# Attention heads and a long convolution in one stream of instructions: another way to order the halves of the fill products, other turns for them, other transfers and another prologue

## The chip, the core and the metric

The kernel runs on one core of a Trainium2 chip. The core has engines that each work through their own list of instructions: TensorE (PE in the profile, with its weight loads as PEld), VectorE (DVE), ScalarE (ACT) and GpSimd (POOL). SyncE (SP) issues transfers; POOL issues some too. The metric is the time of one execution on the device in microseconds (us). Three runs of the kernel before took 1076.99, 1078.38 and 1080.54 us, so the median is 1078.38 us.

## What is computed

There are two independent parts, and the output (1 x 2048 x 1024) is their concatenation. Part A is attention with 32 query heads of 16 dimensions that share one head of keys and values. Part B multiplies a short causal convolution of k (4 taps) by v, applies a causal convolution of length 2048 per channel by a Fourier transform, and gates the result by q. Cut to what matters:

```
# A: x (1,2048,512), wq, wo (512,512), wk, wv (512,16)
q = (x @ wq).reshape(B, S, H, Dh).transpose(0, 2, 1, 3)     # H = 32, Dh = 16
k, v = x @ wk, x @ wv
scores = einsum("bhqd,bkd->bhqk", q, k) * Dh ** -0.5
o = einsum("bhqk,bkd->bhqd", softmax(scores), v)
a = o.transpose(0, 2, 1, 3).reshape(B, S, H * Dh) @ wo
# B: q, k, v (1,2048,512), shift_k (512,4), ssm_k (512,2048), ssm_D (512)
k_shift = sum over t of k_pad[:, t:t+S, :] * shift_k[:, 3 - t]
kv = k_shift * v
y = irfft(rfft(kv, 4096) * rfft(ssm_k, 4096))[:, :2048] + kv * ssm_D
b = q * y
return concatenate([a, b], -1)
```

## The kernel before

The attention sets the frame. Its 32 x 2048 x 2048 scores are cut into 1024 tiles of 128 x 1024, and one tile is one **turn**. 32 turns make a **stack** (4 heads by 512 queries, all keys). In a turn PE makes the scores of a tile (L808: 8 matmuls that use two row halves and four column groups of the array, with 49 rows of contraction: queries in a high and a low part and one row that holds an upper bound of the score), and ACT takes their exponential (L820, `exp`) from a PSUM tile `s` of two banks into SBUF (`p`, 7 buffers). `s` has two buffers. The product with the values (PV, L840, `pv`) comes once in two turns, with 16 matmuls in f32, and adds up in two PSUM banks over a stack. `plan()` fixes the turn of each PV. At a stack's start it delays the first ones: the PV of the first four key pairs stand in four consecutive turns, after four turns without any.

Everything else is **fill**: the query projections, the Fourier products of part B and the output projection. Each is a Python generator (a thread), and `_Fill.turn` decides in each turn of the written program how many fill products PE gets, from the constants `SLOT` (the length of a turn, 916 ns), `SCORES`, `PV`, `UNIT` (prices of the parts) and `LATE` (how far PE may fall behind, 340 ns). The order in which the program is written is the order on each engine; no scheduler changes it.

Fill products run in pairs by `halves()` (L208): one product of a pair uses the upper 64 rows of the array, the other the lower 64, and each writes one of two PSUM banks (pool `pf`, four single banks). Halfway the two change banks. The second half must not write a bank before the last product of the first half has. Before the change the exponential of the next turn carries that wait, so that the PE work of a later turn, which follows that exponential, is ordered too:

```
if half == 0:
    self.mark = y                 # L210ff: the last product of the first half
    yield WAIT, 1, CONT
...
if self.mark is not None:         # exp(), L818ff
    self.tc.add_manual_dep(x.ins, self.mark.ins.name, info, reason="row halves change banks")
```

DVE takes the results out of PSUM and does the radix-4 steps of the transform; its instructions stand in the order of the program too. Transfers go out on two issuing engines: POOL for the tables and inputs of part B, SP for the rest (queries to a DRAM scratch `qd` and back as `st`, attention outputs `od`, weights `wof`, the spilled half `xd` of the transposed x). In `conv_load` (L270), SP issues the transposition of the 4 taps, `skd<-in_B_shift_k`, as a transfer of single elements (2048 x 1 x 1, L274), and POOL's `tpb` (L320) reads the result. The 16 spill transfers (L719) stand in a row at the end of the prologue.

The prologue transposes x in four parts (`x_turn`, L521), projects keys and values (`kv`, L543), projects two groups of queries, and makes the score bound for eight heads (`bound`, L653) before the first two turns. `last` (L1007) ends the program with the last PV, the last head's division (`over`) and the remaining output products `x<-wl,lr` (L206).

## Time and profile before

| what | value |
|---|---|
| median of the runs | 1078.38 us |
| the profiled execution | 1078.28 us |
| its span in the trace | 1076.1 us |
| mean granted PE clock | 0.979 |
| PE busy | 959.0 us, 89% of the span |
| DVE busy | 679.5 us, 63% |
| ACT busy | 971.7 us, 90% |
| POOL busy | 170.8 us, 16% |
| DMA packets, volume | 71985, 83.03 MB |

The span is the time between the first and the last instruction that the profile shows; 2.2 us of the execution lie around it. An engine's busy time is a sum over its instructions, and it tells nothing of which wait ended last. "Idle before" in a row is the time that an engine stood still just before these instructions, and the name behind the arrow is what ended it. PEclk is the share of full clock that TensorE was granted.

### The profile page before, as it was taken

Reading aid. Unit: us, or ns where it says so; the run is one execution under the profiler, and the core shown is the slowest. Engines: PE = TensorE matmul, PEld = TensorE weight load, DVE = VectorE, ACT = ScalarE, POOL = GpSimd, SP = SyncE. Lnnn points to the kernel's source line nnn. Section 1 sums busy time; section 2 is a strip of 40 time slices with the busy share of each in tenths; the row PEclk is TensorE's granted clock in tenths of the full one; section 3 lists DMA queues with packets and bytes.
Section 4 is the critical chain, followed back from the end, with each engine's and each line's share of the span. In section 5 each row is a group of like instructions: output and inputs, shape, how many; then the busy total and the mean of one; then the engine's idle time right before and its main releaser. Section 6 shows DMA issues by size and latency. Waiting matters only on the chain.

```text
span 1076.1 us, 50114 instructions
## 1 busy us (share of the span) xinstructions
PE 959.0 (89%) x22903; PEld 453.9 (42%) x22903; DVE 679.5 (63%) x949; ACT 971.7 (90%) x1038; POOL 170.8 (16%) x300
## 2 busy tenths in 40 slices
PE   6875999899999999989999999999787998999896
PEld 4342444444444444434444444444333443444352
DVE  3607767588826888898888551865998893120142
ACT  3655999899999999999999999999999999999994
POOL 3206221400050000001413112311000001310000
PEclk9887999999999999999999999999999999999998
DMA  7365431722251122212404123421101021220101
GB/s 235 104 15 178 148 103 44 156 59 90 70 112 51 50 70 61 61 40 62 133 27 141 60 88 115 124 77 54 40 20 40 21 70 60 88 93 31 50 4 43
DMA packets 71985, 83.03 MB, mean 77 GB/s; under 512 B 23502, under 2 KB 60952, under 8 KB 71768
## 3 DMA queue, kind: packets, MB, share of 16 engines
q1 hardware_dynamic: 49688, 43.50, 14.6%
q0 software_dynamic: 20320, 35.46, 11.4%
q8 instruction: 181, 2.97, 1.2%
q10 hardware_dynamic: 1760, 0.81, 0.3%
q14 instruction: 36, 0.29, 0.1%
HBM read 54.66 MB, written 25.02 MB: 74 GB/s over the span
## 4 chain that ended last, share of the span: by engine, by line
ACT 40%; PE 38%; issue 11%; DMA 5%; DVE 4%; SPq 0%; ACTq 0%; POOL 0%; DVEq 0%
ACT p L820 40%; PE f L840 16%; PE s L808 10%; PE f L223 10%; DMA skd<-in_B_shift_k 3%; PE f L206 1%; DMA od<-ao 1%; DMA rl<-od 1%; DMA wqf<-in_A_wq 1%; DMA tpb<-skd 1%; DVE sp L144 0%; PE x L529 0%; DVE xT L541 0%; PE x L206 0%; DVE t L354 0%
## 5 line engine op out<-in xcount | busy, mean ns | idle before, releaser
L820 ACT ACTIVATE p<-s 128x1024 f32<-128x1024 f32 x1024 | 959.9, 1049 | 71.6 <-PE s L808 33.5
L840 PE MATMUL f<-p,vx 64*32 64x512 f32 (+1 forms) x8448 | 563.4, 585 | 11.8 <-DVE cut L633 9.2
L808 PE MATMUL s<-st,kst 49*32 49x512 f16 x8192 | 444.5, 383 | 80.3 <-ACT p L820 65.5
L808 PEld LDWEIGHTS <-kst 49*32 49x32 f16 x8192 | 197.1, 90 | 470.2 <-issue 431.3
L840 PEld LDWEIGHTS f<-p,vx 64*32 64x32 f32 x8448 | 171.2, 107 | 58.0 <-issue 24.1
L144 DVE TENSOR_TENSOR sp<-sp 128x1024 f32<-128x1024 f32 x96 | 111.6, 1216 | 0.0
L259 DVE COPY sp<-f 128x512 f32<-128x512 f32 x64 | 41.2, 685 | 85.3 <-PE f L223 85.2
L264 POOL DMA_DIRECT2D ff<-in_ff x64 | 34.2, 539 | 259.9 <-PE s L808 251.9
L851 DVE COPY ao<-f 128x512 f32<-128x512 f32 (+1 forms) x33 | 22.2, 674 | 80.0 <-PE f L840 80.0
L428 POOL DMA_DIRECT2D out<-r x32 | 17.3, 544 | 309.8 <-DVE r L426 309.8
L223 PE MATMUL f<-xT,wq 64*32 64x512 f16 x1344 | 56.6, 382 | 2.6 <-DVE gm L668 2.6
L144 DVE TENSOR_TENSOR sp<-sp,sp 128x1024 f32<-128x1024 f32 x48 | 55.9, 1216 | 0.3
L223 PE MATMUL f<-wo,o 64*32 64x512 f16 x1440 | 55.1, 375 | 0.2 <-DVE gm L668 0.2
L426 DVE TENSOR_TENSOR r<-f,q 128x256 f32<-128x256 f32 x32 | 12.1, 420 | 56.4 <-PE f L223 56.4
L223 PE MATMUL f<-a,ff 64*32 64x256 f32 x1024 | 43.7, 376 | 0.2 <-DVE sp L259 0.2
L223 PE MATMUL f<-hT,ff 64*32 64x256 f32 x1024 | 42.1, 376 | 0.7 <-DVE hT L305 0.7
L223 PE MATMUL f<-sp,fi 64*32 64x256 f32 x1024 | 39.2, 375 | 0.0
L363 DVE TENSOR_TENSOR a<-a,t 128x512 f32<-128x512 f32 x48 | 33.2, 691 | 1.5
L354 DVE TENSOR_TENSOR t<-kk,tpb 128x512 f32<-128x512 f32 (+1 forms) x50 | 33.0, 663 | 1.1 <-DMA kk<-in_B_k 1.1
L223 PEld LDWEIGHTS <-wq 64*32 64x32 f16 x1344 | 25.7, 94 | 17.6 <-DVE gm L668 4.1
L345 POOL DMA_DIRECT2D v<-in_B_v x32 | 17.0, 536 | 96.0 <-PE s L808 48.4
L223 PEld LDWEIGHTS <-o 64*32 64x32 f16 x1440 | 23.4, 93 | 14.7 <-issue 3.3
(133 smaller groups left out, 643.1 us busy)
## 6 DMA issues: line engine op xcount, KB each, us to landing
ff<-in_ff POOLq DMA_DIRECT2D x64, 128.0 KB, 2.9
od<-ao SPq DMA_DIRECT2D x60, 128.0 KB
qd<-qp SPq DMA_DIRECT2D x48, 128.0 KB
st<-qd SPq DMA_DIRECT2D x60, 98.0 KB
kk<-in_B_k POOLq DMA_DIRECT2D x32, 128.0 KB, 3.1
v<-in_B_v POOLq DMA_DIRECT2D x32, 128.0 KB, 2.5
hin<-in_B_ssm_k POOLq DMA_DIRECT2D x32, 128.0 KB, 7.4
fi<-in_fi POOLq DMA_DIRECT2D x32, 128.0 KB, 2.8
```

The costliest lines, as they stand in the source:

```text
L144: v.tensor_tensor(part(out), part(a), part(b), op)
L223: y = self.nc.tensor.matmul(out[j : j + 32, cols], w[r, j : j + 32], x[r], start=half == m == 0, stop=half == 1 and m == k - 1,)
L259: self.nc.vector.tensor_copy(c[:, :, m + i, :], b[i].rearrange("p (q n) -> p q n", q=2))
L264: self.nc.gpsimd.dma_start(t[:, i], self.I[n][:, 2 * m2 + i])
L345: nc.gpsimd.dma_start(v[:, i], self.vr[:, 2 * m2 + i, cs])
L354: nc.vector.tensor_tensor(out[:, n], kk[:, x], tap(i, n.stop - n.start), ALU.mult)
L363: nc.vector.tensor_tensor(a, a, t, ALU.add)
L428: nc.gpsimd.dma_start(self.orr[:, 2 * m2 + i, D + blk * CB : D + (blk + 1) * CB], r[:, i])
L808: self.nc.tensor.matmul(s[j : j + 32, e, :], self.kst[rows, k * P + j : k * P + j + 32], self.st[n][rows, a, cols], start=True, stop=True,)
L820: x = self.nc.scalar.activation(self.pt[u], s, AF.Exp, scale=DH**-0.5 / SC / SC)
L840: nc.tensor.matmul(self.acc[e][32 * j : 32 * j + 32, 0:m], self.vx[rows, k, :], y, start=k == 0, stop=k == NKT - 1)
L851: nc.vector.tensor_copy(a, self.acc[0][:, 0:m])
```

## The change

The change has these parts.

- **Halves.** `halves()` no longer sets a mark for the exponential. After the first half it writes a tiny DVE instruction, a memset of a 128 x 4 tile `look`, that waits for the last product of the first half; the first product of the second half waits for the memset. The two banks of a pair now come as one PSUM tile (`pair()`, two buffers in the place of four single banks), and the wait between the halves is one turn in the place of two.
- **Turns.** `LATE` goes from 340 to 200, so a turn with PV has no room for fill. `plan()` puts a stack's first PV two turns late and the second in two parts of 256 columns, one and three turns late. The exponential is written straight behind the scores.
- **Transfers.** The taps are loaded as rows of 128 elements, transposed by a DVE copy and written to `skd` in rows of 32. `ssm_D` comes as 8 rows of 32 with a DVE transposition. The 16 spill transfers become a thread `spill` with one per turn, and the reloads, the loads of part B and those of the heads are spread in the same way; the convolution waits for the end of `spill`.
- **Prologue.** Matmuls of zeros (`warm`) stand at the start and in gaps. PSUM places of the x transposition alternate between both pools. The score bound of the first stack's four heads is written straight into `st` (row 32 of each row half, `first_rows`); only the first 256 keys are prepared before the first scores, and the second group of queries, the keys from 1024 on and the second stack move behind the first turns into `rest_of_q`.

```diff
-SLOT, SCORES, PV, UNIT, LATE = 916, 220, 430, 216, 340
+SLOT, SCORES, PV, UNIT, LATE = 916, 220, 430, 216, 200
...
-LEAD = 44
+LEAD = 30
...
+    def pair(self):
+        return self.pf.tile([P, 2, 512], F32, tag="f", name=self.nm("f"))
     def bank(self):
-        return self.pf.tile([P, 512], F32, tag="f", name=self.nm("f"))
+        return self.pair()[:, 0, :]
+    def order(self, a, b):
+        info = mybir.DependencyInfo(mybir.DependencyClass.Sync, mybir.DependencyReason.DATA)
+        self.tc.add_manual_dep(a.ins, b.ins.name, info, reason="row halves change banks")
...
-        banks = []
+        banks, look = [], None
         for half in range(2):
             n, k = 0, len(a)
             while n < k:
                 g = yield (k - n) * grain, dve * half, CONT if banks else NEW, grain
                 start = not banks
                 if start:
-                    banks += [self.bank(), self.bank()]
+                    f = self.pair()
+                    banks += [f[:, 0, :], f[:, 1, :]]
                 for m in range(n, n + g // grain):
                     for e in range(2):
                         out, (cols, w, x) = banks[half ^ e], (a, b)[half ^ e][m]
@@ -227,10 +236,14 @@
                                 start=half == m == 0,
                                 stop=half == 1 and m == k - 1,
                             )
+                            if look is not None:
+                                self.order(y, look)
+                                look = None
                 n += g // grain
             if half == 0:
-                self.mark = y
-                yield WAIT, 1, CONT
+                look = self.nc.vector.memset(self.look, 0.0)
+                self.order(look, y)
+                yield WAIT, 0.5, CONT
         return banks
...
-        self.dt = self.c.tile([32, 8], F32, name="dt")
+        sk = w.tile([16, 32, 4], F32, tag="s2", bufs=S2, name="sk")
+        nc.sync.dma_start(sk, I["B_shift_k"].rearrange("(c h) t -> c h t", c=16))
         self.skd = self.dr.tile([4, 512], F32, name="skd")
-        nc.sync.dma_start(self.skd, I["B_shift_k"].rearrange("c t -> t c"))
         yield WAIT, 6
+        tps = w.tile([16, 4, 32], F32, tag="s2", bufs=S2, name="tps")
+        yield 0, 200
+        nc.vector.tensor_copy(tps, sk.rearrange("c h t -> c t h"))
+        nc.sync.dma_start(self.skd.rearrange("t (c h) -> c t h", c=16), tps)
...
-        self.nc.sync.dma_start(self.dt, self.I["B_ssm_D"][blk * CB : blk * CB + CB].rearrange("(c p) -> p c", p=32))
...
+            yield WAIT, 1.5
...
+        d = [self.s2("d", (32,)) for _ in range(2)]
+        nc.gpsimd.memset(d[0][0:32], 0.0)
+        nc.sync.dma_start(d[0][0:8], self.I["B_ssm_D"][blk * CB : blk * CB + CB].rearrange("(c p) -> c p", p=32))
         yield WAIT, 4
-        yield 0, 200
-        d = hin[0:32, :, 0:1]
-        nc.vector.tensor_tensor(d, d, self.dt.unsqueeze(2), ALU.add)
+        yield 0, 400
+        nc.vector.transpose(d[1][0:32], d[0][0:32])
...
         yield from self.conv_load()
+        yield from self.after("spill")
         self.sp, self.kv2 = {}, {}
-        self.ld[0] = self.short_load(0)
+        yield from self.short_load(0)
         yield from self.short(0)
-        hin = self.long_load(0)
+        hin = yield from self.long_load(0)
...
+    def warm(self, b, x, n):
+        for _ in range(n):
+            self.nc.tensor.matmul(b, x[:, 0:P], x, start=True, stop=True)
...
+    def first_bound(self, b, a):
+        nc = self.nc
+        for e in range(2):
+            h = e + 2 * a
+            r = slice(BR + 64 * e, BR + 64 * e + 1)
+            nc.tensor.matmul(b[r, e, :], self.wb[:, h : h + 1], self.qa[0, 0], start=True, stop=True)
+    def first_rows(self, b, st, a):
+        f = -1.02 * SC * SC / ONE
+        for e in range(2):
+            r = slice(BR + 64 * e, BR + 64 * e + 1)
+            self.nc.vector.tensor_scalar(st[r, a, :], b[r, e, :], f, -60000.0, ALU.mult, ALU.max)
...
+        warm = lambda b, n: self.warm(b[:, 1, :], zero, n)
+        warm(self.pair(), 10)
+        self.wb_cut()
+        self.x_turn(0, [self.wide() for _ in range(2)])
         nc.scalar.mul(self.wq[0][:, 0], self.wqf[0], WS)
         nc.vector.scalar_tensor_tensor(self.wq[0][:, 1], self.wqf[0], WS, self.wq[0][:, 0], ALU.mult, ALU.subtract)
-        self.x_turn(0)
-        self.x_turn(1)
+        far = [self.pair() for _ in range(2)]
+        warm(far[1], 4)
+        far += [self.wide()]
+        self.x_turn(1, far, lambda: warm(far[2], 3))
+        self.x_turn(2, [far[2], self.pair()])
+        b = self.wide()[:, 0, :]
         for dk in range(4):
-            self.q_mm(0, 0, b, dk)
-        self.q_out(0, 0, b, True)
+            for i, (_, w, x) in enumerate(self.three(self.wq[0][:, :, dk, :], self.xT[0][:, :, dk, :])):
+                nc.tensor.matmul(b, w, x, start=dk == i == 0, stop=dk == 3 and i == 2)
+        cut = self.q_cut(b)
+        self.x_turn(3, [self.pair(), self.wide()], cut=cut)
         for g in range(1, 4):
             self.parts(nc.gpsimd, self.wq[g][:, 0], self.wq[g][:, 1], self.wqf[g], WS)
-        self.x_turn(2)
-        self.x_turn(3)
-        kv = self.kv()
-        st = [self.stack(n, 48) for n in range(2)]
-        rows = self.kv_rows(kv)
-        self.k_max(kv)
-        b = self.bank()
-        cut = [self.k_cut(0, rows[0])]
-        self.bound(0, 0, b, st)
-        b1 = self.bank()
-        for dk in range(4):
-            self.q_mm(1, 0, b1, dk)
-        self.k_rows(0, cut[0])
-        cut += [self.k_cut(c, rows[c]) for c in range(1, 4)]
-        self.bound_max(0, 0, b)
+        st = self.stack(0, True)
+        b = self.wide()[:, 0, :]
+        self.kvt = kv = self.kv(b)
+        scr = self.wide()
+        warm(scr, 2)
+        rows = self.pair()
+        self.kv_rows(kv, 0, rows[:, 0, :])
+        rest = self.k_max(scr[:, 0, :])
+        warm(scr, 2)
+        n = 256
+        cut, h16 = self.k_cut(rows[:, 0, :], 0, n)
+        nc.scalar.copy(h16, cut)
+        rest()
+        b = self.pair()
+        self.first_bound(b, 0)
+        self.k_rows(0, cut, h16, 0, n)
+        self.first_rows(b, st, 0)
+        warm(scr, 3)
+        self.v_turn(kv, scr[:, 0, :])
         self.exp(0, self.scores(0))
+        self.first_bound(b, 1)
+        self.first_rows(b, st, 1)
+        self.kv_rows(kv, 1, rows[:, 1, :])
         self.exp(1, self.scores(1))
-        self.v_turn(kv)
-        self.k_rows(1, cut[1])
-        self.q_out(1, 0, b1)
+        cut, h16 = self.k_cut(rows[:, 0, :], n, n)
+        nc.vector.tensor_copy(h16, cut)
+        self.k_rows(0, cut, h16, n, n)
+        self.k_chunk(1, rows[:, 1, :])
+        nc.gpsimd.tensor_scalar(self.gm[:, 16:17], self.km, self.cut, 0.0, ALU.mult, ALU.add)
+    def k_chunk(self, c, b):
+        cut, h16 = self.k_cut(b)
+        self.nc.vector.tensor_copy(h16, cut)
+        self.k_rows(c, cut, h16)
+    def spill(self):
         for c in range(2, 4):
-            self.k_rows(c, cut[c])
             for i in range(8):
-                nc.sync.dma_start(self.xd[c - 2, :, i // 4, i % 4], self.xT[c][:, i // 4, i % 4])
+                yield WAIT, 0.5
+                self.nc.sync.dma_start(self.xd[c - 2, :, i // 4, i % 4], self.xT[c][:, i // 4, i % 4])
+        self.seen.add("spill")
+        for c in range(2):
+            yield from self.after(f"q{c}")
+            for i in range(8):
+                yield WAIT, 1
+                self.nc.sync.dma_start(self.xT[c + 2][:, i // 4, i % 4], self.xd[c, :, i // 4, i % 4])
+            self.seen.add(("x", c + 2))
...
-        x = self.nc.scalar.activation(self.pt[u], s, AF.Exp, scale=DH**-0.5 / SC / SC)
-        if self.mark is not None:
-            info = mybir.DependencyInfo(mybir.DependencyClass.Sync, mybir.DependencyReason.DATA)
-            self.tc.add_manual_dep(x.ins, self.mark.ins.name, info, reason="row halves change banks")
-            self.mark = None
-    def pv(self, x):
+        self.nc.scalar.activation(self.pt[u], s, AF.Exp, scale=DH**-0.5 / SC / SC)
...
-            plan.setdefault(x + 1 + max(0, 3 - x // 2 % NKT), []).append(x)
+            k = x // 2 % NKT
+            if k == 1:
+                for part, late in enumerate((1, 3)):
+                    plan.setdefault(x + 1 + late, []).append((x, part))
+            else:
+                plan.setdefault(x + 1 + 2 * (k == 0), []).append((x, None))
         for x in range(last, 2 * NQ * NKT):
-            plan.setdefault(x + {0: 2, 1: 1, 2: 1}.get(x % NKT, 0), []).append(x)
-        cost = {i: sum(2 if x < last else 1 for x in v) for i, v in plan.items()}
+            plan.setdefault(x + {0: 2, 1: 1, 2: 1, 3: 1}.get(x % NKT, 0), []).append((x, None))
+        cost = {i: sum(2 if x < last and part is None else 1 for x, part in v) for i, v in plan.items()}
...
-            if t % 32 == 12 and 2 <= t // 32 + 1 < NQ:
+            if t % 32 == (22 if t < 32 else 12) and t // 32 + 1 < NQ:
                 self.stack(t // 32 + 1)
-            s = self.scores(t)
+            self.exp(t, self.scores(t))
             self.step, self.slot = x // 2, x
             for y in plan.get(x, []):
-                self.pv(y)
+                self.pv(*y)
             fill.turn(x, cost.get(x, 0), cost.get(x + 1, 0))
-            self.exp(t, s)
```

Three places show how the order of the instructions moves.

The first is SP's list of transfers behind the prologue. `xd` is the spill, `wof` an output weight, `skd` the taps in DRAM, `gn` a score bound, `od` an attention output. Before:

```order
14 L651 DMA qd<-qp_461 8x16x512 x3
15 L719 DMA xd<-xT 128x512 x16
16 L919 DMA wof_505<-in_A_wo 128x512
17 L274 DMA skd<-in_B_shift_k 2048x1x1
18 L665 DMA qd<-gn_668 8x512
19 L919 DMA wof_675<-in_A_wo 128x512
20 L919 DMA wof_937<-in_A_wo 128x512
21 L919 DMA wof_1202<-in_A_wo 128x512
22 L855 DMA od<-ao_1246 128x256 x2
```

Now:

```order
14 L1026 DMA wof_415<-in_A_wo 128x512
15 L286 DMA sk<-in_B_shift_k 16x128
16 L792 DMA xd<-xT 128x512 x7
17 L693 DMA qd<-gn_566 8x512
18 L792 DMA xd<-xT 128x512 x2
19 L1026 DMA wof_614<-in_A_wo 128x512
20 L792 DMA xd<-xT 128x512 x2
21 L292 DMA skd<-tps 16x4x32
22 L792 DMA xd<-xT 128x512 x5
23 L871 DMA st_805<-qd 49x2x512 x2
```

The transfer of 2048 single elements is gone, the taps go out in rows between spill transfers, and the spill stands in pieces between the others.

The second is DVE at the first Fourier products (`sp` takes the results of a pair of products out of PSUM; `a`, `t` and `cut` are results of the short convolution and of the queries). Before:

```order
74 L244 SCALAR_TENSOR_TENSOR wo_1204<-wof_1202,wo_1204 128x512
75 L252 TENSOR_REDUCE gx<-wo_1204 128x1
76 L354 TENSOR_TENSOR t_1389<-kk_713,tpb_708 128x512
77 L363 TENSOR_TENSOR a_1326<-a_1326,t_1389 128x512
78 L259 COPY sp_725<-f_1444 128x2x256
79 L259 COPY sp_725<-f_1445 128x2x256
```

Now:

```order
66 L666 TENSOR_SCALAR cut_1566<-f_986 128x512
67 L387 TENSOR_TENSOR a_1532<-a_1532,t_1546 128x512
68 L244 MEMSET look 128x4
69 L378 TENSOR_TENSOR t_1629<-kk_780,tpb_779 128x512
70 L387 TENSOR_TENSOR a_1532<-a_1532,t_1629 128x512
71 L378 TENSOR_TENSOR t_1671<-kk_780,tpb_779 128x512
72 L387 TENSOR_TENSOR a_1532<-a_1532,t_1671 128x512
73 L389 TENSOR_TENSOR a_1532<-a_1532,v_1529 128x512
74 L272 COPY sp_968<-f_1600 128x2x256 x2
```

A memset now stands in DVE's list between the halves of each such pair, 67 in all, behind whatever DVE has before it.

The third is DVE between the key projection and the first scores (`km` the largest key, `kc`, `kh`, `kst` the parts of the keys, `wb` the weights of the score bound, `gn` the bound). Before:

```order
11 L596 TENSOR_REDUCE km<-kv 128x1
12 L598 TENSOR_SCALAR kx<-msk,km 128x4
13 L602 TENSOR_REDUCE kmr<-f_347 128x1
14 L608 TENSOR_SCALAR wb<-msk,kmr 128x32
15 L609 TENSOR_SCALAR wb<-msk 128x8
16 L610 TENSOR_SCALAR gm<-km 128x1
17 L571 TENSOR_SCALAR kc_356<-x_337,msk 128x512
18 L659 TENSOR_SCALAR gn_359<-f_355 8x512
19 L578 CAST kh_418<-kc_356 128x512
20 L580 SCALAR_TENSOR_TENSOR kst<-kh_418,msk,kc_356 128x512
```

Now:

```order
12 L593 TENSOR_REDUCE km<-x_273 128x1
13 L628 TENSOR_SCALAR kx<-msk,km 128x4
14 L605 TENSOR_SCALAR kc_336<-f_329,msk 128x256
15 L633 TENSOR_REDUCE kmr<-x_326 128x1
16 L634 TENSOR_SCALAR wb<-msk,kmr 128x8
17 L612 SCALAR_TENSOR_TENSOR kst<-kh_338,msk,kc_336 128x256
18 L709 TENSOR_SCALAR st_268<-f_343 1x512 x4
```

Three instructions (the second `wb`, `gm`, and `kh`) left DVE's list for POOL and ACT, the keys are prepared 256 at a time, and the bound is written into `st` itself, two rows before the first scores and two behind them.

More of the change, by code (lines that the diff above doesn't have):

```diff
@@ L28 @@
 KR = 49
+BR = 32
 XS, WS = 16.0, 16.0
@@ L537, in x_turn @@
                 turn(dp, rows)
+            if rows.start == 0:
+                between()
         for dp in range(2):
@@ L726, in hurry, with bounds @@
         return 4 if any(self.step >= x and ("wo", 4 * c) not in self.seen for c, x in enumerate(WO_AT)) else None
-    def rest_of_q(self):
-        for g in range(4):
-            yield 0, 700
-            self.guard(self.wq[g][:, 0])
-        yield 0, 200
-        self.guard(self.wkv[:, 0])
+    def bounds(self, g, c):
+        yield 2, 1400, NEW, 2
+        b = self.bank()
+        self.bound(g, c, b)
+        self.bound_max(g, c, b)
+        self.qs.add((g, c))
+    def rest_of_q(self):
+        for c in range(2, 4):
+            yield 1, 2000, NEW, 1
+            b = self.bank()
+            self.kv_rows(self.kvt, c, b)
+            self.k_chunk(c, b)
+        yield from self.bounds(0, 0)
+        work = [y for dk in range(4) for y in self.three(self.wq[1][:, :, dk, :], self.xT[0][:, :, dk, :])]
+        n = 0
+        while n < 12:
+            g = yield 12 - n, 1400, CONT if n else NEW, 1
+            if n == 0:
+                b = self.bank()
+            for m in range(n, n + g):
+                self.mm(b, *work[m][1:], start=m == 0, stop=m == 11)
+            n += g
+        yield from self.q_parts(1, 0, self.q_cut(b))
         for c in range(4):
+            if c > 1:
+                yield from self.after(("x", c))
             for g in (0, 2):
@@ L747, in rest_of_q @@
                     yield WAIT, 2
-                    yield 2, 1400, NEW, 2
-                    b = self.bank()
-                    self.bound(h, c, b)
-                    self.bound_max(h, c, b)
-                    self.qs.add((h, c))
+                    yield from self.bounds(h, c)
+            if c == 0:
+                for g in range(4):
+                    yield 0, 700
+                    self.guard(self.wq[g][:, 0])
+                yield 0, 200
+                self.guard(self.wkv[:, 0])
             yield 0, 2200
```

169 lines of the change are left out of this document (86 added, 83 removed).

## The prediction

> **What bounds the kernel now.** I began with the page's busy shares and its slices.
>
> ```profile
> PE 959.0 (89%) x22903; PEld 453.9 (42%) x22903; DVE 679.5 (63%) x949; ACT 971.7 (90%) x1038; POOL 170.8 (16%) x300
> ...
> ACT  3655999899999999999999999999999999999994
> PEclk9887999999999999999999999999999999999998
> ```
>
> PE and ACT are both near 90%. The slices show where ACT is not: it is weak in the first four slices (27 us each) and full from the fifth on. Next came the groups of instructions, and the longest pieces of the timeline in which ACT ran without a gap.
>
> ```profile
> L820 ACT ACTIVATE p<-s 128x1024 f32<-128x1024 f32 x1024 | 959.9, 1049 | 71.6 <-PE s L808 33.5 <-PE f L223 26.1 <-remote 8.0
> ...
> 808.06 14.18 ACT L820 ACTIVATE p<-s 128x1024 f32<-128x1024 f32 x15
> ...
> 869.42 35.42 ACT L820 ACTIVATE p<-s 128x1024 f32<-128x1024 f32 x38 [0.26 <-PE f L223]
> ```
>
> The 1024 exponentials are the frame. One lasts 1.049 us, but they overlap: 38 in 35.42 us give a pitch of (35.42 - 1.05) / 37 = 0.929. Where nothing else presses, the starts in the timeline lie 0.912 apart (the median). So 1023 pitches of 0.912 = 933.0 us are the floor of the kernel's body, and what the change can win is what stands above it. I split the span by windows over the exponential's line alone.
>
> ```profile
> 36.46:122.60 86.14, 60.49 (x64) 0.86 0.58 123
> 122.60:1059.40 936.80, 898.45 (x961) 0.99 0.24 69
> ```
>
> (The columns are the window, its length, ACT's busy time and count in this line, granted clock, DMA share, GB/s.) The first exponential starts at 36.46. The first 64 take 86.1 us where 64 x 0.912 = 58.4 would do: 27.8 us lost. The other 959 pitches, up to the start of the last at 1059.4, take 936.8, where 959 x 0.912 = 874.6: 62.2 lost. From there to the end are 1076.1 - 1059.4 = 16.7. The profiled execution took 1078.28, so 2.2 lie outside the span. Sum: 36.5 + 933.0 + 27.8 + 62.2 + 16.7 + 2.2 = 1078.4, which is the median of the runs too; the forecast is made against that.
>
> Which waits make the losses, by the table of waits (total, count, longest):
>
> ```profile
> ACT p L820 <- PE s L808: 33.5, 23, 10.4
> ACT p L820 <- PE f L223: 26.1, 63, 1.9
> ACT p L820 <- remote: 8.0, 3, 3.4
> POOL tpb L320 <- DMA skd<-in_B_shift_k: 46.2, 1, 46.2
> PE f L840 <- DVE cut L633: 9.2, 2, 8.7
> DVE sp L259 <- PE f L223: 85.2, 22, 12.2
> ```
>
> **The change, term by term.**
>
> *The first 64 turns (27.8 lost).* The windows, SP's timeline and the chain that ended last belong together here.
>
> ```profile
> 57.00:79.00 22.00, 16.52 (x296) 8.53 (x280) 0.00 (x0) 10.76 (x12) 0.00 (x0) 0.84 0.63 12
> 90.00:100.00 10.00, 5.80 (x64) 2.81 (x72) 9.76 (x18) 1.63 (x2) 6.73 (x13) 0.50 0.70 216
> ...
> 51.72 0.72 SPq L274 DMA_DIRECT2D skd<-in_B_shift_k  x1
> 52.54 17.88 SPq L665 DMA_DIRECT2D qd<-gn  x1
> ...
> 51.72 28.23 DMA skd<-in_B_shift_k
> ...
> q1 hardware_dynamic: 1521, 0.23, 61.1%
> q8 instruction: 2, 0.03, 1.7%
> ```
>
> (In the windows the pairs are PE, PEld, DVE, ACT and POOL.) From 57 to 79 the DMA engines are 63% busy and move only 12 GB/s: these are the 2048 single elements of the taps, 61.1% for 1521 packets of 0.23 MB (the queues of this window are the last two rows). They hold SP's next issue for 17.88 us, `skd` lands after 28.23, and DVE does nothing. ACT makes 12 exponentials in 22 us, 22 - 12 x 0.912 = 11.1 us lost. Its three waits on "remote" (8.0) lie there, and the two packets of the instruction queue took 1.7% of 16 engines x 22 us, some 6.0 us: I read this as PE and ACT short of instructions behind the elements. The second loss is from 90 to 100, 10.4 us in one wait: PE stands 8.7 us for `cut`, which on DVE stands behind `t`, which waits for `kk` and `tpb`, which wait for `skd`. With rows in place of elements both go. The new transfers (16 rows, 16 x 4 rows of 32) are of the size of `qd<-qp`, and the spill's 16 pieces spread over 16 turns. What replaces them: the new prologue leaves more to the first turns (two key chunks, a bound, the 12-product query projection with its 4.28 us, below), and DVE's `cut` can still be late. I take 27.8 down to 5, between 1 (all gone) and 16 (the first stall stays).
>
> [...]
>
> *The prologue (36.46).* Rows around its end:
>
> ```profile
> 28.27 0.59 ACT kv L557
> 28.91 1.14 PE x L565 x8
> ...
> 31.77 4.28 PE f L206 x48
> ...
> 36.46 1.94 ACT L820 ACTIVATE p<-s 128x1024 f32<-128x1024 f32 x2 [7.61 <-PE s L808]
> ...
> 28.89 0.69 DVE L596 TENSOR_REDUCE km<-kv 128x1 f32<-128x512 f32 x1 [1.46 <-ACT kv L557]
> 32.03 0.67 DVE L659 TENSOR_SCALAR gn<-f 8x512 f16<-8x512 f32 x1
> 33.06 1.53 DVE L580 SCALAR_TENSOR_TENSOR kst<-kh,msk,kc 128x512 f16<-128x512 f16 x1
> ```
>
> From the end of the key projection (28.27) to the first exponential are 8.2 us, with 4.28 of the second query group on the path. Now `km` reads PSUM and need not follow the copy of 0.59; the second group is behind. Left on the chain: `km` 0.69, `kx` and the two small products about 0.8, `kc` at half size 0.4, `wb` 0.3, `kst` at half size some 0.7, two bound rows at 0.67 each, scores 0.4, together 4.6 and about 0.6 between them. That is 5.2 in place of 8.2, so 33.5. Ahead of 28.27 the projection and the transposes can use more PSUM places and fewer instructions stand on DVE; the warm products cost PE time only where it waits anyway. I put that at 1.5 us, between -3.5 (nothing there is on the path but the transfers of x) and +1.5 (the zeros are in the way). First exponential: 32.0, between 29 and 36.
>
> *The later losses (62.2).* They have four parts, each with its row.
>
> First, the mark: 26.1 us in 63 waits of the exponential for the first half (`PE f L223`). It goes, since the exponential no longer waits there. What takes its place is the look. PE's second half waits for DVE, and behind it in PE's order stand the next scores. The second half now comes two turns (1.83 us) after the first ends in 56 of 67 places, and one turn after it in 11. DVE is mostly ahead, by the 85.2 us that it waits for the last product in the row above. So 56 cost nothing unless two long instructions stand ahead, and 11 cost up to one instruction. DVE's largest are these:
>
> ```profile
> L144 DVE TENSOR_TENSOR sp<-sp 128x1024 f32<-128x1024 f32 x96 | 111.6, 1216 | 0.0
> ```
>
> I take 11 x 0.2 = 2 us; the ends are 0 and 67 x 1.2 = 80.
>
> Second, PV at a stack's start. Four in a row, where each holds a PE turn of 1.08:
>
> ```profile
> 817.65 1.05 PE L840 MATMUL f<-p,vx 64*32 64x512 f32 x16
> 818.51 0.41 PE L808 MATMUL s<-st,kst 49*32 49x512 f16 x8
> 818.73 1.05 PE L840 MATMUL f<-p,vx 64*32 64x512 f32 x16
> ```
>
> 817.65 to 818.73 is 1.08, or 0.16 above the pitch; about 70 turns are so, 11 us. (15 exponentials in 14.18 us, above, are this place: pitch 0.938.) The new plan never has two whole PVs in neighbouring turns, so I take all 11.
>
> Third, the clock at the same place. One of five such drops:
>
> ```profile
> 780.00:790.00 10.00, 7.79 (x136) 2.81 (x125) 8.78 (x10) 8.80 (x10) 0.00 (x0) 0.83 0.15 48
> ...
> 786.37 1.97 PE L840 MATMUL f<-p,vx 64*32 64x512 f32 x16
> 788.88 1.02 ACT L820 ACTIVATE p<-s 128x1024 f32<-128x1024 f32 x1 [1.10 <-PE s L808]
> ```
>
> Four turns in which PE has only scores precede it; the granted clock falls to 0.83 in that window, the PV takes 1.97 where 1.05 is usual, and ACT stands still for 1.10; by its starts it loses 1.8 there, and five times that is 9 us. Now it is three turns, and fill stands in most of them: I take 9, between 0 and 9.
>
> [...]
>
> Fourth, the rest, 62.2 - 26.1 - 11 - 9 = 16: turns where fill and PV together exceed two pitches, DVE late at the output banks, transfers. Turns with PV no longer take fill, so about half of the over-full ones go: by the order of PE's work, pairs of turns above 1.83 us fall from 44 to 10. But DVE's own stalls stay, and each pair now holds both of its banks until both are read: 12 stay. Later losses: 2 + 12 = 14, between 5 and 60.
>
> *The end (16.7).* The last fill now ends about twelve turns later, and its two DVE reads and the division of the third quarter stand closer to the end:
>
> ```profile
> 1060.13 1.07 PE L206 MATMUL x<-wl,lr 128*32 128x512 f32 x8
> 1061.13 0.66 PE L840 MATMUL f<-p,vx 64*32 64x256 f32 x16
> ...
> 1062.82 0.45 DVE L999 STREAM_TRANSPOSE lb<-ao 128x256 f32<-128x256 f32 x1
> 1064.55 0.42 DVE L1005 TENSOR_TENSOR lb<-ao,lb 128x256 f32<-128x256 f32 x1
> ...
> L988 DVE TENSOR_TENSOR wp<-wp,f 128x512 f32<-128x512 f32 x4 | 2.6, 684 | 5.9 <-PE f L223 5.9
> ```
>
> `x<-wl,lr` stands before the last PV on PE. A division is six DVE instructions, from 1062.82 to 1064.97 in these rows, 2.15. By two `wp` at 0.68 ahead of it, and a third of this already done when the last exponential ends, `lr` comes about 2 us behind the last exponential. So 16.7 + 2.0 = 18.7, between 16.7 and 20.
>
> **Sum.** 32.0 + 933.0 + 5 + 14 + 18.7 + 2.2 = 1004.9 us; I forecast 1005.
>
> **The rivals.**
>
> *The looks cost what the marks did.* If DVE is mid-row in the transform when the first half ends, PE waits in most places, and the 67 looks cost 0.4 us each: 27 in place of 2, 1030 us. For it: DVE is 63% busy, with rows of 1.2 us. Against it: the two turns of slack.
>
> *The stall of 57 to 79 stays,* because the instruction queue is hit by the load of that time as such (the spill, the tables), or because it had another cause: 1005 + 11 = 1016. The clock drops that stay give 1014, about the same.
>
> *Slower: PE waits at the look.* DVE works in order, and a look behind an instruction that waits for a transfer or for PE's own other results holds PE, and with it the scores. It decides from (1081.6 - 1005 + 2) / 67 = 1.17 us a look. A look must then land 3.0 us behind its half where the slack is 1.83, so with 2.5 of DVE's longest instructions ahead of it. For it: DVE waited 8.7 us for transfers in one place already. Against it: DVE reads a finished bank about 0.1 us behind PE in most places of this trace.
>
> *More is won:* the prologue at 29, losses of 1 + 5 and an unchanged end: 29 + 933 + 6 + 16.7 + 2.2 = 987.
>
> **How the numbers follow.** The forecast has 0.60, the stall or the clock drops that stay 0.13, the costly looks 0.12, more won 0.05, and the slower case 0.10, of which 0.02 fall within 0.3% (3.2 us, about what a measurement of this kernel can tell from no change). So faster 0.90, same 0.02, slower 0.08. The range leaves out the slower case and half of the fullest gain: 985 to 1040; the forecast's own range is 995 to 1015.
>
> **What would show it.** Right: no `remote` wait and no window of 12 GB/s; `skd` lands within some 3 us; the first exponential near 32; no wait of the exponential on the fill's line; 64 exponentials within 64 us; no 1.97 us PV after a stack's start; the end 2 us longer. Wrong: a wait of PE's fill on the `look` line in the table of waits beyond 10 us, a first stack that still takes 40 us, or DVE late at the banks so that PE waits for a pair.

## The result and the profile after

The changed kernel takes 1040.32 us (median of 4 runs, 1038.94 to 1042.55); the kernel before took 1079.46 in the runs beside it. The ratio is 0.964, with a 95% interval of 0.961 to 0.967. So 39 us of the forecast 73 were won, and the time lies just outside the range (985 to 1040). One run of e2 below, 1063.74 us, was in a slower state and is left out of its times; all other runs count.

The page of the changed kernel: busy shares, the slices of ACT, and the exponential's group with its line by shape.

```profile
PE 956.9 (92%) x23391; PEld 466.4 (45%) x23391; DVE 686.1 (66%) x1023; ACT 960.1 (92%) x1040; POOL 171.2 (16%) x305
...
ACT  4599998899997999999999989999999999999983
...
L921 ACT ACTIVATE p<-s 128x1024 f32<-128x1024 f32 x1024 | 947.6, 1067 | 42.3 <-PE s L909 39.5 <-ACT p L921 0.7
```

Of the four weak slices at the start two are left, and ACT's idle time falls from 71.6 to 42.3 us. But the 7th, 8th and 13th slices (26 us each: 156 to 208 and 312 to 338 us) stand at 8, 8 and 7 tenths, and the 24th and 39th at 8, where the slices before had one 8 between the fourth and the last. Nearly all of ACT's idle time (39.5 us) is now put down to the scores: PE was late with them. The same split as in the prediction, by windows over the exponential's line (window, length, ACT busy and count, clock, DMA share, GB/s):

```profile
32.54:98.39 65.85, 60.00 (x64) 0.91 0.42 125
98.39:1021.22 922.83, 886.51 (x959) 0.99 0.25 73
```

| term | forecast | after | with the look on POOL (below) |
|---|---|---|---|
| first exponential starts | 32.0 | 32.5 | 30.7 |
| floor, 1023 pitches of 0.912 | 933.0 | 933.0 | 933.0 |
| first 64 turns, above 58.4 | 5 | 7.5 | 7.4 |
| the other 959, above 874.6 | 14 | 48.2 | 21.8 |
| start of the last exponential to the end | 18.7 | 19.3 | 20.5 |
| outside the span | 2.2 | 2.1 | 2.1 |
| sum (profiled execution) | 1004.9 | 1042.6 | 1015.4 |

Four terms came within 3 us. One is wrong by 34 us: the losses behind the first two stacks. The table of waits shows what PE was late for (total, count, longest):

```profile
DVE look L244 <- PE f L232: 80.5, 26, 7.3
ACT p L921 <- PE s L909: 39.5, 29, 5.7
PE f L232 <- DVE look L244: 18.9, 11, 4.9
PEld f L232 <- DVE look L244: 16.2, 7, 5.3
```

(The row of PEld is of the weight loads at these looks; it is not added to that of PE.) In 26 of 67 cases DVE stood ready at the look and waited for PE. In the other 41 no such wait is listed: the look came up behind DVE's other work. In most of them PE still had something else to do; it stood still at 11 looks, for 18.9 us in all. A usual case of the 11 in the timeline, DVE first, then PE:

```profile
159.92 0.69 DVE L952 COPY ao<-f 128x512 f32<-128x512 f32 x1
160.65 0.69 DVE L953 TENSOR_TENSOR ao<-ao,f 128x512 f32<-128x512 f32 x1
161.25 0.68 DVE L378 TENSOR_TENSOR t<-kk,tpb 128x512 f32<-128x512 f32 x1
161.97 0.69 DVE L387 TENSOR_TENSOR a<-a,t 128x512 f32<-128x512 f32 x1
162.59 0.68 DVE L378 TENSOR_TENSOR t<-kk,tpb 128x512 f32<-128x512 f32 x1
162.61 0.06 DVE L244 MEMSET look<- 128x4 f32 x1
...
162.74 1.10 PE L232 MATMUL f<-a,ff 64*32 64x256 f32 x32 [2.04 <-DVE look L244]
```

The memset itself takes 62 ns. It stands behind at least eight DVE instructions of about 0.69 us without a gap (these five and three before them), and PE stands still for 2.04 us. The longest case is at 310 (the first two rows are of the chain that ended last):

```profile
302.73 7.23 DMA r<-rd
309.96 2.58 issue
...
312.54 0.69 DVE L1016 TENSOR_TENSOR o<-of,r 128x512 f16<-128x512 f32 x1 [6.46 <-issue]
313.26 0.69 DVE L1016 TENSOR_TENSOR of<-of,r 128x512 f32<-128x512 f32 x1
313.99 0.69 DVE L1016 TENSOR_TENSOR o<-of,o 128x512 f16<-128x512 f32 x1
314.63 0.06 DVE L244 MEMSET look<- 128x4 f32 x1
314.76 1.10 PE L232 MATMUL f<-hT,ff 64*32 64x256 f32 x15 [4.89 <-DVE look L244]
```

There the look stands behind `o`, which needs the transfer `r`. That transfer takes 7.23 us and lands at 309.96, about when PE comes to a stand (314.76 - 4.89 = 309.87). Then DVE does not start for another 2.58 us, in which the trace names nothing that it waits for ("issue"), and its three products take 2.1. So PE's 4.89 us are mostly that halt and these products, and only through DVE's lateness the transfer.

### The profile page after: what moved, and what is told of

It reads as the page before. It is cut to its first block, busy times and chain, and to the rows that moved or that the text cites. A ratio compares the mean times of both kernels' runs of the same rounds, so it can differ in the third digit from the quotient of the medians.

```text
span 1040.5 us, 51057 instructions
## 1 busy us (share of the span) xinstructions
PE 956.9 (92%) x23391; PEld 466.4 (45%) x23391; DVE 686.1 (66%) x1023; ACT 960.1 (92%) x1040; POOL 171.2 (16%) x305
## 4 chain that ended last, share of the span: by engine, by line
ACT 46%; PE 33%; issue 9%; DVE 8%; DMA 3%; SPq 0%; ACTq 0%; DVEq 0%
ACT p L921 46%; PE f L941 15%; PE s L909 9%; PE f L232 7%; DVE sp L152 2%; DMA rd<-rl 1%; DMA r<-rd 1%; DVE ao L952 1%; DVE ao L953 1%; DMA xb<-in_A_x 1%; PE f L600 1%; DVE sp L272 1%; DVE a L387 1%; DVE t L378 0%; DMA qd<-qp 0%
## 5 line engine op out<-in xcount | busy, mean ns | idle before, releaser
L921 ACT ACTIVATE p<-s 128x1024 f32<-128x1024 f32 x1024 | 947.6, 1067 | 42.3 <-PE s L909 39.5
L909 PE MATMUL s<-st,kst 49*32 49x512 f16 x8192 | 431.3, 385 | 37.2 <-ACT p L921 33.9
L941 PEld LDWEIGHTS f<-p,vx 64*32 64x32 f32 x8944 | 179.6, 107 | 37.2 <-issue 10.4
L244 DVE MEMSET look<- 128x4 f32 x67 | 4.2, 62 | 80.5 <-PE f L232 80.5
L232 PE MATMUL f<-xT,wq 64*32 64x512 f16 x1344 | 51.6, 376 | 5.1 <-DVE gm L712 2.6
```

The source lines that it names most:

```text
L232: y = self.nc.tensor.matmul(out[j : j + 32, cols], w[r, j : j + 32], x[r], start=half == m == 0, stop=half == 1 and m == k - 1,)
L909: self.nc.tensor.matmul(s[j : j + 32, e, :], self.kst[rows, k * P + j : k * P + j + 32], self.st[n][rows, a, cols], start=True, stop=True,)
L921: self.nc.scalar.activation(self.pt[u], s, AF.Exp, scale=DH**-0.5 / SC / SC)
L941: nc.tensor.matmul(self.acc[e][32 * j : 32 * j + 32, m], self.vx[rows, k, :], y, start=k == 0, stop=k == NKT - 1)
```

## The experiments

Theory: the looks stand in DVE's order, and PE with the scores behind it waits for DVE's list. Rival: the losses come from the output banks that are held in pairs, from the turns without room, or from transfers, and the waits at the looks only show them. All times are medians beside runs of the kernel before on the same chip, which lay at 1078.9 to 1079.5 us each time.

**e1, the look on POOL.**

```diff
-                look = self.nc.vector.memset(self.look, 0.0)
+                look = self.nc.gpsimd.memset(self.look, 0.0)
```

> The look between the halves is written by POOL in place of DVE; nothing else changes. Theory (the looks stand in DVE's order, and PE waits for DVE's queue): the losses behind the first stack fall from 48 us to some 20, PE's wait for the look from 19 to under 3, and the time goes from 1040 to 1010 to 1018. Rival (the losses come from the output banks that are held in pairs, or from the turns without room, and the wait for the look only shows where PE would wait anyway): 1035 to 1042.

Measured: 1014.19 us (1012.15 to 1015.41), ratio 0.938 (0.934 to 0.943). That is 26 us below the changed kernel by one word. Its exponentials by windows, and its waits:

```profile
30.69:96.42 65.73, 60.01 (x64) 0.92 0.40 121
96.42:992.82 896.40, 885.25 (x959) 1.00 0.25 75
...
POOL look L244 <- PE f L232: 681.3, 57, 107.5
ACT p L921 <- PE s L909: 14.2, 16, 2.1
```

In 57 of 67 cases POOL is ready and waits for PE. The losses of the 959 turns fall from 48.2 to 21.8, and the other terms move by less than 2 us. The output banks are still held in pairs here and the turns are the same, so these parts of the rival fall. What is left open by this run: POOL's list now has waits in it, so POOL's transfers start later too (the row of eight `hin` at 309.90 in place of 299.92). The paced run below separates that.

**e2, the taps by single elements again** (and e11 the same with the look on POOL).

```diff
-        nc.sync.dma_start(sk, I["B_shift_k"].rearrange("(c h) t -> c h t", c=16))
         self.skd = self.dr.tile([4, 512], F32, name="skd")
+        nc.sync.dma_start(self.skd, I["B_shift_k"].rearrange("c t -> t c"))
...
-        nc.vector.tensor_copy(tps, sk.rearrange("c h t -> c t h"))
-        nc.sync.dma_start(self.skd.rearrange("t (c h) -> c t h", c=16), tps)
```

> The taps are transposed by single elements again, as before the change; the rest is as after. Theory of the prediction (the elements hold up the queue and the instruction stream): a window of some 20 us with 12 GB/s and a DMA share over 0.5 comes back, ACT loses about 11 us in it and about 10 more where the first convolution waits, so 1050 to 1062. Rival (the stall had another cause): within 4 us of 1040.

> Look on POOL and the taps by single elements. This is the price of the elements without the looks: if it is the stall in the first stack, 9 to 12 us over 1014, all of it before the first 64 exponentials are done, with a wait on the instruction stream. If the elements only shift where looks meet DVE's work: 1012 to 1018.

Measured: e2 1055.31 us (1047.87 to 1057.61), 15 above the changed kernel; in its profile the first 64 exponentials take 75.3 us in place of 65.9. e11 1025.36 (1024.03 to 1028.98), 11 above the look on POOL alone. Of e11, the two windows of exponentials, SP's issues, ACT's wait, and three engines at 65 us:

```profile
30.63:109.26 78.63, 60.98 (x64) 0.91 0.55 101
109.26:1002.86 893.60, 884.74 (x959) 1.00 0.25 76
...
28.81 33.26 SPq L787 DMA_DIRECT2D xd<-xT  x7
...
ACT p L916 <- remote: 3.7, 2, 2.6
...
65.15 0.42 PE L904 MATMUL s<-st,kst 49*32 49x512 f16 x3 [1.89 <-issue]
65.22 0.69 DVE L661 TENSOR_SCALAR cut<-f 128x512 f32<-128x512 f32 x1 [14.88 <-remote]
65.37 2.85 ACT L916 ACTIVATE p<-s 128x1024 f32<-128x1024 f32 x3 [2.55 <-remote]
```

The first 64 exponentials take 78.6 in place of 65.7: 12.9 us, and nothing is lost behind them. So the price of the elements is that first stall. They hold SP's next seven issues for 33.26 us, where the changed kernel has 3.36, and the wait on "remote" is back, 3.7 us in two waits. The rival, that the stall had a cause other than the elements, falls. By what they stop the engines is not shown. At 65 us PE stops in the middle of the eight products of a score with nothing named, and PE, DVE and ACT go on within 0.22 us of each other. What "remote" is, the table doesn't say. (DVE's 14.88 us are for the most part a wait for `f`, which PE finishes only after 61 us; in the changed kernel the same `cut` waits 8.79 us for it.) The 10 us of the second loss (`cut` behind `tpb`) don't come back. The convolution now starts behind `spill`, which may be why; no run separates it.

**e3 and e12, no matmuls of zeros,** with the look on DVE and on POOL: the loop of `warm` runs 0 times.

```diff
-        for _ in range(n):
+        for _ in range(0):
```

> The matmuls of zeros in the prologue are left out. If they keep the clock up: the first exponential 2 to 4 us later, 1042 to 1045. If PE waits there anyway and the clock does not matter: within 1 us of 32.5 and of 1040, or a little earlier.

> Look on POOL and no matmuls of zeros in the prologue. If the clock in the prologue matters: 1016 to 1019. If not: 1012 to 1016.

Measured: 1037.96 (1035.98 to 1046.1) against 1040.3, and 1018.93 (1014.08 to 1023.34) against 1014.2. The medians part in opposite directions and the runs overlap. The first exponential starts at 30.9 and 30.2 in the profiles, not later than with the zeros (32.5 and 30.7; between 30.6 and 32.5 in the other profiles), and with the look on POOL the first 64 take 66.1 us without the zeros and 65.7 with them. So they gain nothing that these runs can show.

**e4 and e7, `LATE` 340 again,** with the look on DVE and on POOL.

```diff
-SLOT, SCORES, PV, UNIT, LATE = 916, 220, 430, 216, 200
+SLOT, SCORES, PV, UNIT, LATE = 916, 220, 430, 216, 340
```

> LATE is 340 again, so turns with PV take fill again; the rest is as after. If the over-full turns mattered as the prediction has it: 5 to 15 us slower than 1040. If DVE's order is the main loss: within 5 us, since looks then stand elsewhere in DVE's list but wait the same.

> Look on POOL, and LATE 340. With the looks out of DVE's order the price of over-full turns stands by itself. The prediction put it at about 4 us (16 to 12): 1015 to 1022. If fill in the turns with PV costs nothing: within 3 us of 1014.

Measured: 1038.53 (1035.89 to 1042.26), the same as the changed kernel, and 1023.18 (1018.86 to 1026.97), 9 us above the look on POOL alone. Its profile has one halt like that at 65 us in e11, again in the middle of a score's products, while POOL's transfers `hin` and `ff` keep the DMA engines 89% busy (203 to 210 us):

```profile
209.16 0.40 PE L909 MATMUL s<-st,kst 49*32 49x512 f16 x4 [3.63 <-issue]
```

This and single waits are in the 9 us, so what the over-full turns cost by themselves is not shown; it may well be the forecast's 4. Under the looks on DVE nothing of it can be seen. There, I take it, the looks meet other work when the fill stands elsewhere.

**e5, the heads' products later.** Only the products that need `r` are written eight turns later.

```diff
-        yield WAIT, 2
+        yield WAIT, 6 if G < 12 else 2
         for out, a, b, op in ((oc[:, 0], o, r, ALU.mult), (o, o, r, ALU.mult), (oc[:, 1], o, oc[:, 0], ALU.subtract)):
```

> The looks stay on DVE; the three products of a head group with its reciprocal sums (L1016) are written eight turns later in all groups but the last four, so that their transfer has landed. If the longest stalls are looks behind a DVE instruction that waits for a transfer: the stall of 4.9 us at the look near 310 and the turns behind it (about 8.3 us in that stack) go, 1029 to 1034, and PE's wait for the look falls from 19 to some 12. If DVE's own work stands ahead of the looks: within 4 us of 1040.

Measured: 1041.23 us (1036.51 to 1042.9), no gain. The waits at the looks fell as expected (18.9 to 11.2 on PE), but the stall near 310 stayed, without the look. Its timeline and the window's DMA queues (packets, MB, share):

```profile
304.02 0.06 DVE L244 MEMSET look<- 128x4 f32 x1 [2.63 <-PE f L232]
310.26 0.43 PE L232 MATMUL f<-hT,ff 64*32 64x256 f32 x2 [4.65 <-issue]
...
305.00:310.20 5.20, 0.61 (x21) 0.14 (x9) 0.00 (x0) 1.42 (x2) 2.62 (x4) 1.00 0.80 143
...
q0 software_dynamic: 2495, 1.11, 81.9%
```

The look is done at 304.02, and PE stops in the middle of a group of products and waits for nothing that the trace names. At that time POOL issues the 16 transfers `hin` in a row, in packets of some 450 B that take 81.9% of the DMA engines' time (the last row is for 303 to 311 us). The trace shows the load and the halt, not the link. In the changed kernel DVE's 2.58 us of "issue" fall under the same transfers (79.3% in 303 to 311 us). So at this place a second cause stood beside the look, and moving the products alone gained nothing.

**e9, POOL held back, the look on DVE.**

```diff
-                look = self.nc.vector.memset(self.look, 0.0)
+                look = self.nc.vector.memset(self.look[:, 0:2], 0.0)
                 self.order(look, y)
+                self.order(self.nc.gpsimd.memset(self.look[:, 2:4], 0.0), y)
```

> The look stays on DVE and PE waits for it there; POOL gets a memset of its own behind the same product, for which nobody waits, so that POOL's list of transfers is held back as with the look on POOL. If DVE's order is the loss: 1036 to 1042, as after. If POOL's transfers, which start earlier without a look in POOL's list, are the loss: 1012 to 1018. If both: between, with the stall near 310 gone and those of 1 to 3 us at the looks left, 1024 to 1034.

Measured: 1035.32 us (1033.0 to 1036.13). The waits of its looks:

```profile
DVE look L244 <- PE f L232: 78.1, 27, 6.6
PE f L232 <- DVE look L244: 13.8, 9, 2.0
```

The long look near 310 is gone (the longest is 2.0 in place of 4.9), those of 1 to 2 us are not. Both memsets wait for the same product, so this run shows how late DVE is. One place:

```profile
437.52 0.69 DVE L954 TENSOR_TENSOR ao<-ao,f 128x512 f32<-128x512 f32 x1
437.53 0.10 POOL L246 MEMSET look<- 128x2 f32 x1 [28.14 <-PE f L232]
438.12 2.36 DVE L152 TENSOR_TENSOR sp<-sp 128x1024 f32<-128x1024 f32 x2
439.29 0.06 DVE L244 MEMSET look<- 128x2 f32 x1
439.42 1.40 PE L232 MATMUL f<-hT,ff 64*32 64x256 f32 x24 [1.77 <-DVE look L244]
```

POOL's memset runs as soon as the product is done, DVE's 1.76 us later, behind the readout of a finished stack (`ao`) and two instructions of the transform. Of the 26 us between the changed kernel and the look on POOL, some 5 come from POOL's transfers (a difference the intervals hardly part) and 21 from DVE's order; the profiles agree, with 48.2, 41.8 and 21.8 us lost in the 959 turns.

**e6, PV four in a row again,** with the look on POOL.

```diff
-            if k == 1:
-                for part, late in enumerate((1, 3)):
-                    plan.setdefault(x + 1 + late, []).append((x, part))
-            else:
-                plan.setdefault(x + 1 + 2 * (k == 0), []).append((x, None))
+            plan.setdefault(x + 1 + max(0, 3 - x // 2 % NKT), []).append((x, None))
```

> Look on POOL, and the PV of a stack's start stand four in a row again, after four turns without. The kernel beside it is that with the look on POOL alone, 1014. The prediction's terms: 11 us for turns of 1.08 and up to 9 for the clock, so 1020 to 1034. If neighbouring turns take that up: within 4 us of 1014.

Measured: 1040.72 us (1038.79 to 1041.22), 26.5 above the look on POOL alone. Of this, three single stalls cost 16 in the starts of the exponentials; two are looks behind POOL's own transfers (the second of 2.56 us, at 870), one a table that came late. I put these down to where the fill now falls; no run separates that from PV:

```profile
558.84 1.11 PE L232 MATMUL f<-sp,fi 64*32 64x256 f32 x16 [3.70 <-POOL look L244]
605.61 0.98 PE L232 MATMUL f<-a,ff 64*32 64x256 f32 x12 [3.13 <-DMA ff<-in_ff]
...
777.27 1.95 PE L941 MATMUL f<-p,vx 64*32 64x512 f32 x16
779.41 1.45 PE L941 MATMUL f<-p,vx 64*32 64x512 f32 x16
...
774.00:784.00 10.00, 8.21 (x144) 2.90 (x151) 9.86 (x11) 8.39 (x10) 0.00 (x0) 0.83 0.24 77
```

The other 10 lie at the starts of the stacks themselves. The clock drop is back (PV of 1.95 and 1.45 behind the turns without PV, a granted clock of 0.83), which the look on POOL with the new plan doesn't show: its granted clock over the 959 turns is 1.00.

**e8 and e10, the end, with the look on POOL** (e8 with the heads later as well).

```diff
-        self.mm(s[0], rows(self.lr, 0), self.wl[1])
         self.pv(2 * NQ * NKT - 1, None)
+        self.mm(s[0], rows(self.lr, 0), self.wl[1])
```

> Look on POOL, the heads' products later, and at the end the last PV ahead of the output product that waits for the division. Against 1014: the heads 0 to 2 us (nothing waits behind them any more), the end 3 us, since DVE can read the last PV as soon as its division of the third quarter is done: 1009 to 1012. If the end is bound by DVE's division anyway: 1013 to 1015.

> Look on POOL and the last PV ahead of the output product that waits for the division; the heads as they were. The time from the last exponential's end to the end of the span falls from 19.4 (look on POOL alone) to some 14.2, so 1007 to 1011. If the end gives this back elsewhere: 1013 to 1016.

Measured: e10 1011.82 us (1008.59 to 1015.86), the fastest of all by its median, ratio 0.937 (0.933 to 0.941); e8 1021.55 (1017.15 to 1022.59). In both profiles the last exponential's end lies 14.2 us before the span's end, where the look on POOL alone has 19.4: the last PV no longer stands behind a product that waits for the division. By the medians the gain is 2.4 us, within the spread of the runs. e8 gives back 10 us; with the heads later, a table comes late and PE stands still for 3.09 of them, and the rest is not put down to a place.

```profile
994.42 0.67 PE L941 MATMUL f<-p,vx 64*32 64x256 f32 x16 [0.25 <-ACT p L921]
996.33 0.42 DVE L952 COPY ao<-f 128x256 f32<-128x256 f32 x1
996.51 1.92 PE L214 MATMUL x<-wl,lr 128*32 128x512 f32 x16 [1.43 <-issue]
...
595.65 1.18 PE L232 MATMUL f<-a,ff 64*32 64x256 f32 x12 [3.09 <-DMA ff<-in_ff]
```

The first three rows are of e10: the last PV runs right behind the exponential, DVE reads it at 996.3, and the output product follows. The last row is of e8.

## Why the prediction was wrong

- **The looks: the step that failed.** The prediction put them at 11 x 0.2 = 2 us, with ends of 0 and 80. They cost some 21 in DVE's order, and 26 with POOL's transfers, which start earlier when no look stands in POOL's list (the row of eight `hin` at 299.92, against 310.86 in e9). The argument was that DVE is "mostly ahead", by the row in which DVE waits 85.2 us for the last product. That row has 22 waits for 64 copies: it says that DVE was ahead in a third of the places, and nothing of the rest. The looks behave the same way, 26 of 67.
- **It had the number of dear places and not their price.** PE stood still at 11 looks, as many as the prediction priced, but for 1.7 us each and not 0.2. Nine of the 11 lie at the same point: the start of a stack, where DVE has just read the finished stack's result (`ao`, two of 0.69 us) and mostly has other work behind that. There the second half also follows at once. With the look on POOL it starts 0.15 to 0.24 us behind the start of the memset in these nine places, and 0.8 to 1.3 us behind it in nearly all others. So the slack of 1.83 us was too high nearly everywhere, and at a stack's start there was none. Ahead of the look, in place of "up to one instruction", stood the readout and up to three more. (These 18.9 us are not all of the cost; where the rest of it arises is open.)
- **Its rival that the looks cost what the marks did** had the price nearly right, 27 in place of 2, at a chance of 0.12. Its picture, 0.4 us in most places, was not right. Its 1030 us lie ten short of the measured time because of the rest of the later losses, below.
- **Its slower rival** shows in one place in part: at 310 DVE was late by a transfer, but PE's halt there is mostly DVE's 2.58 us without a named cause and its three products.
- **The elements: right.** The stall of the first stack was forecast at 11.1, and e11 has 11.2 by the medians and 12.9 in the first 64 turns. Beside the elements ACT waits 3.7 us on "remote" and PE stops for 1.89 us in the middle of a score; that they were short of instructions there, as the prediction reads it, no run shows.
- **The first 64 turns: 7.5 against 5,** right in kind. The table of waits has no "remote" left; 5.9 of what is left lies in the first seven turns, in which PE has key chunks to do between the scores.
- **The start: 32.5 against 32.0, by two errors that cancel.** The key projection was over at 24.7, not 26.8, but the chain from there took 7.9 us and not 5.2. The row of the prologue shows one of its gaps: DVE waits 1.57 us for the product of the key rows (`kc`), which was not counted.

```profile
24.66 0.69 DVE L593 TENSOR_REDUCE km<-x 128x1 f32<-128x512 f32 x1 [0.68 <-PE x L584]
27.18 0.54 DVE L605 TENSOR_SCALAR kc<-f,msk 128x256 f32<-128x256 f32 x1 [1.57 <-PE f L600]
32.55 1.02 ACT L921 ACTIVATE p<-s 128x1024 f32<-128x1024 f32 x1 [0.16 <-PE s L909]
```

- **PV and the clock at a stack's start: right in kind, about half in size.** Forecast 20, of which e6 shows some 10 apart from its stalls. With the look on POOL the clock drops went with the plan (1.00 over the 959 turns) and came back with the old one (0.83 in the 10 us from 742 and from 774). The term of 9 counted five drops. The trace of before has three behind the first 120 us (a granted clock of 0.83 in the 10 us from 200, from 780 and from 1000; 1.00 in all other windows between 120 and 1060), and two of them stand behind turns with scores alone, 0.41 us of PE in each 0.92. In the changed kernel itself the drop still comes, behind the long looks: a PV of 2.01 us at 164.35 and of 1.95 at 727.30, with a granted clock of 0.83 in the 10 us from 160 and from 725.
- **The rest of the later losses, 12, was short too.** With the look on POOL 21.8 are left. That is the ten by which the costly-looks case misses, and about what PV and the clock were taken too high. Part is the pitch itself: its median rose from 0.912 to 0.915, some 3 us, which the floor didn't allow for.
- **The transfers "one per turn" are not that on the chip.** The prediction counted the spill as 16 pieces over 16 turns. SP issues seven within 3.36 us and five within 3.74, since nothing in its list waits for a turn. It did no harm there that these runs show. POOL's `hin` in a row stands beside the halts at 310.

```profile
32.34 3.36 SPq L792 DMA_DIRECT2D xd<-xT  x7
```

- **The end: 19.3 against 18.7,** right, with its cause: with `LATE` 340 (e4 and e7), where the last fill ends earlier, it is 16.7 and 17.0.

## What to carry to other kernels

A tiny instruction that only passes on an order costs what stands ahead of it in its engine's list: here 62 ns of its own, and 1.7 us of PE at each of 11 looks. So it belongs on the engine that is idle when it is due, and "how often did this engine wait here" is read from the count of the waits beside the count of the instructions, not from their sum. A wait that is taken from one engine and given to another should be priced in the list of the new one, at the places where it stands, with the longest run of work that this list has there and with the slack that is left there, not with an average. Here one place, the start of a stack, took nine of the eleven halts. And a transfer that is written later in the program starts later only where something in its issuer's list waits: seven spill transfers, written one per turn, went out within 3.36 us.

## What the runs showed of the hardware

With 2048 transfers of one element on a queue, SP's next seven issues took 33.26 us in place of 3.36, and PE, DVE and ACT stood still and went on within 0.22 us of each other (e11, at 65 us), ACT for 2.55 us with no wait of the program named. Two more places of this kind lie beside POOL's transfers. With 2495 packets of 445 B on average in 8 us, PE halted for 4.65 us in the middle of a group (e5), and in e7 for 3.63 us in the middle of a score. The link between the load and the halt is not shown. The memset of 128 x 4 took 62 ns on DVE and 102 ns on POOL, and yet POOL was the better place by 21 us, because of what stood ahead of it on DVE. The granted clock fell to 0.83 in 10 us behind turns in which PE had 0.41 us of scores in each 0.92 us (780 to 790 before). Matmuls of zeros ahead of the first real ones made no difference that the runs can tell (without them 1037.96 against 1040.32 us with the look on DVE, and 1018.93 against 1014.19 with it on POOL).
